# A gated mix of recurrent attention and a GEGLU FFN on one core: down weights in six narrower buffers, turns of x in four banks, earlier first fills, later moved loads, fewer closing waits

## The chip, the cores and the metric

The kernel runs on one core of one Trainium2 chip. The core has engines with instruction streams of their own: TensorE (PE, with its weight loads PEld), VectorE (DVE), ScalarE (ACT), GpSimd (POOL) and SyncE (SP, which here only issues transfers). They share an on-chip buffer and eight accumulation banks of 128 x 512 fp32, numbered 0 to 7. A DMA is issued by an engine (SP, ACT or POOL), and a semaphore says when it has landed. An engine works its stream in order: an instruction that waits holds up everything behind it on that engine.

The metric is the time of one execution on the device in microseconds; less is better. Before the change it is 2202.14 us, the median of 3 runs (2199.84 to 2203.8).

## The reference

Inputs are x (1 x 2048 x 1024), a start memory of 8 rows, attention weights for 32 heads of 128, FFN weights with F = 3584, and gate_w; all bf16. The result mixes a recurrent attention `a` with a feed-forward block `b` by a gate per row:

```python
def _A_ref(x, mem0, Wq, Wk, Wv, Wo, seg_len):          # seg_len 32: 64 segments
    mask = (idx[:, None] < M) | (idx[:, None] >= idx[None, :])
    mem = mem0
    for s in range(n_seg):
        h = jnp.concatenate([mem, xs], axis=1)         # 8 + 32 rows
        q, k, v = (jnp.einsum('btd,dhe->bhte', h, W) for W in (Wq, Wk, Wv))
        scores = jnp.einsum('bhqe,bhke->bhqk', q, k) * scale
        p = _softmax(jnp.where(mask[None, None], scores, -1000000000.0), axis=-1)
        o = jnp.einsum('bhqk,bhke->bhqe', p, v)
        o = jnp.einsum('bhte,hed->btd', o, Wo)
        mem = o[:, :M, :].copy()                       # the next segment's memory
        outs.append(o[:, M:, :])
    return jnp.concatenate(outs, axis=1)

def _B_ref(x, w_gate, w_up, w_down):
    return _gelu(x @ w_gate) * (x @ w_up) @ w_down

g = _sigmoid((x * gate_w).sum(-1, keepdims=True))
return g * a + (1 - g) * b
```

Each segment's memory is the output of the one before it, so the 64 steps are a chain. The three `einsum`s for q, k, v are written as one line here.

## The kernel before

**How the program comes about.** The source builds a list with `op(engine, function, rd=..., wr=..., lane=...)`. From what an operation reads and writes a small planner works out what it must wait for. A `lane` is a semaphore that counts one kind of DMA. There is no scheduler: each engine gets its operations in the order in which the source calls `op`. `emit` writes the streams; at the end SP waits for every lane's last value (`finals`, line 153), 98 lanes in 49 instructions. On POOL each operation that is no DMA waits for the one before it, too.

**FFN first** (loop over `fb`, lines 1053 to 1164): four blocks of 512 tokens. The up phase runs over j = 0 to 27, slices of 128 of F: 8 matmuls with w_gate and 8 with w_up into two banks (line 1068), then gelu and the product on ACT and DVE (1076 to 1084) into `GT[j]`. The down phase has two passes, `ps` = 0 and 1, of two 128-token tiles each, four matmuls per j (line 1134). In blocks 0 to 2 the down weights come in pieces of `WD` = 4 slices (1 MB) through three buffers `wd0` to `wd2`. The first pass takes the pieces forward, the second backward (`back`), so that the last ones are still there. When a piece is done, its buffer is loaded with the piece three further on; in the backward pass at c = 3 SP first issues `load_xT`, the next block's x, turned. In block 3 all down weights lie in `wdF`, filled during its up phase by the table `jF`.

**Turns of x** (`do_x`, 546 to 575): for each 128-token tile T eight transposes on PE write a bank; ACT and DVE copy the bank to `xT` or `xq`; a third copy on DVE takes the 8 last rows of each segment to `hR`, `hR1` or `xr`; `put` writes both to the scratch tensors `xq_scr` and `xr_scr` with DMAs issued by ACT. `dot_x` makes the gate's dot product for T: a product on POOL and a reduction on DVE, one right behind the other. `gate(fb)` turns four of them into sigmoids and stores them to `gt_scr`. Tiles 0 to 3 are turned at the start, later ones in j = 6, 11, 16, 21 of blocks 0 to 2. `tr_mem` transposes the start memory and part of the mask, at the start too.

**The scan** (64 steps) holds what it can of the attention weights in 50 slots of 512 KB, `edge(n)` being the start of slot n. What does not fit is swapped in each step, by SP: a 1.5 MB and a 1 MB load for v, 1 MB each for k and q, and pieces of Wo (`wall`). `walk` is the fixed order of the 64 weight pieces in a step: k, q and v with r = 0, k and q with r = 1, o with r = 0, v with r = 1, o with r = 1, eight numbers n each; r is the half of the heads. `plan(s)` hangs operations on places of the walk: `on("q", 1, 4, f)` runs f just before piece ("q", 1, 4). `begin(n)` issues the first load of slot n, as soon as its bytes in the FFN's layout are free.

For the 8 rows that a segment passes on, keys, queries and values of their x part are worked out ahead for four segments at a time: `fill` (line 907) projects them with a weight half that lies in the slots, `fill_evac` copies the bank to a stage (`X0` to `X3`, `Y0` to `Y2`) and, for v, writes it to `v_scr` (`v_scr puts`, by POOL); `fill_put` turns k or q and writes it to `qk_scr`, by POOL too. Before they are used POOL reads them back: `load_qk` into `qkr`, `load_v` into `vB`. `put_rest` (936) copies the keys from `qkr` behind those of the step (`kT`). `scores` (757) needs this; `attend` has two parts, the second (800) reading `vB`. For step 0 all of these come early: k and q of half 0 in the FFN's last pass, the others in step 0 itself. POOL's order there was load_v(0, half 0), kT copy, fills' stores, load_qk(0, 1), kT copy, load_v(0, half 1).

**The end.** In the last step five Wo pieces, which the closing reads again, are loaded to other places (`late`, lane names moved0 to moved4). The closing (line 1189) multiplies what `o_scr` collected for the 512 passed-on rows (`oR0` to `oR3`, 128 rows each) with Wo, 32 matmuls per half of the columns; DVE mixes (1197) into `orb`, and SP stores it. `blend` mixes the other rows, tile by tile, and ACT stores them. A store of the second half writes the same key `("D", "out", T)` as that of the first, so it waits for it.

The five lines on which the down phase's waits hang:

```python
if back and c == 3:
    load_xT(fb + 1)
nc_ = c - 3 if back else c + 3
if 0 <= nc_ < NWD:
    load_wd(nc_)
```

## Time and profile before

| what | time, us |
| --- | --- |
| median of 3 runs | 2202.14 (2199.84 to 2203.8) |
| profiled execution, own time | 2196.2 |
| its span, first to last instruction | 2194.4 |
| x loaded and turned, first up matmul starts | 11.2 |
| block 0: up, down | 102.56, 53.87 |
| block 1: up, down | 101.36, 49.39 |
| block 2: up, down | 100.42, 50.44 |
| block 3: up; down with the first fills | 96.91; 54.8 |
| step 0 of the scan starts, about | 625 |
| closing, first to last matmul of line 1189 | 2131.27 to 2187.1 |
| last out store issued | 2190.42 |

An "own time" is the device time of the one execution that the profiler took; the span runs from its first to its last instruction, and 1.8 us lie around it. The 64 steps take about 22.9 us each, some 1,506 of the 2,194 us. Over the whole span the page has these totals:

```profile
PE 2033.8 (93%) x31337; PEld 972.6 (44%) x31365; DVE 1027.1 (47%) x2657; ACT 551.6 (25%) x1142; POOL 443.1 (20%) x835
...
DMA packets 180106, 640.23 MB, mean 292 GB/s; under 512 B 25144, under 2 KB 74936, under 8 KB 138976
...
wd<-in_B_w_down_dram SPq DMA_DIRECT2D x27, 1024.0 KB, 6.7
```

The first line gives each engine's busy time, its share and its number of instructions: TensorE is busy for 93% of the span. The last is from the list of DMA issues: 27 loads of down weights of 1 MB, with a median of 6.7 us from issue to landing.

### The profile page before, as it was taken

The page shows a single profiled execution, that of the slowest core. Times are in us where ns is not written, and L with a number is a line of the kernel's source. Part 1 is how long each engine was busy: PE and PEld are TensorE (multiplying, and loading weights), DVE is VectorE, ACT ScalarE, POOL GpSimd, SP SyncE. Part 2 cuts the span into 40 slices and gives each one's busy share as a digit, 9 for nine tenths or more (in the row PEclk, how much of TensorE's full clock was granted, in tenths as well). Part 3 has the DMA queues.
Part 4 walks back from the last instruction along what each step waited for, and adds up shares of the span by engine and source line. Part 5 has one row for each costly group of instructions (what it writes and reads, how often), then busy time and mean ns, then how long its engine had stood idle before and what let it go on. Part 6 is the DMA issues. An engine that isn't in the chain of part 4 may idle for free.

```text
span 2194.4 us, 69744 instructions
## 1 busy us (share of the span) xinstructions
PE 2033.8 (93%) x31337; PEld 972.6 (44%) x31365; DVE 1027.1 (47%) x2657; ACT 551.6 (25%) x1142; POOL 443.1 (20%) x835
## 2 busy tenths in 40 slices
PE   8999999999979899998999999999899999999878
PEld 4444444444434444444444444444444444444345
DVE  5615616436224445444454454544544545445444
ACT  3303303213112222222222222222223222222210
POOL 3000100000022222322223223222232322222110
PEclk9999999999999999999999999999999999999999
DMA  9352264364587999999899999999999999999997
GB/s 308 128 192 89 91 219 124 84 234 165 185 307 285 336 338 344 346 358 345 328 357 348 356 354 342 356 343 360 344 340 349 346 338 358 337 348 347 337 334 269
DMA packets 180106, 640.23 MB, mean 292 GB/s; under 512 B 25144, under 2 KB 74936, under 8 KB 138976
## 3 DMA queue, kind: packets, MB, share of 16 engines
q1 hardware_dynamic: 150800, 595.52, 74.3%
q0 software_dynamic: 17472, 26.41, 3.9%
q10 hardware_dynamic: 11536, 13.85, 1.8%
q8 instruction: 246, 4.03, 0.7%
q14 instruction: 52, 0.43, 0.1%
HBM read 600.00 MB, written 50.27 MB: 296 GB/s over the span
## 4 chain that ended last, share of the span: by engine, by line
PE 65%; DMA 22%; DVE 6%; ACT 3%; issue 2%; POOL 1%; ACTq 0%; SPq 0%; POOLq 0%
PE pb L834 24%; PE pb L1068 14%; DMA wall<-o_scr 9%; PE pb L1134 7%; PE pb L850 5%; PE pb L732 3%; PE pb L867 3%; PE pb L907 3%; PE pb L1189 3%; DMA o_scr<-oRc 2%; DMA sl<-v_scr 2%; DMA wd<-in_B_w_down_dram 2%; DMA qk_scr<-1S 2%; DVE oT L718 1%; DMA v_scr<-kS 1%
## 5 line engine op out<-in xcount | busy, mean ns | idle before, releaser
L834 PE MATMUL pb<-sl,hT 128*32 128x512 bf16 x12288 | 761.8, 382 | 21.4 <-DVE hT L894 8.8
L834 PEld LDWEIGHTS pb<-sl,hT 128*32 128x32 bf16 x12288 | 309.4, 97 | 328.1 <-DVE hT L894 27.6
L907 PE MATMUL pb<-sl,hR 128*32 128x512 bf16 x3072 | 213.5, 384 | 7.1 <-DMA sl<-in_A_Wk_dram 3.8
L1068 PE MATMUL pb<-xT,wg 128*128 128x512 bf16 x896 | 213.4, 381 | 5.4 <-DVE GT L1084 4.1
L1068 PE MATMUL pb<-xT,wu 128*128 128x512 bf16 x896 | 212.5, 380 | 0.0
L817 POOL COPY oRc<-oT 128x128 bf16<-128x128 bf16 x128 | 96.6, 755 | 407.6 <-DVE oT L718 407.6
L867 PE MATMUL pb<-wall,oT 128*32 128x256 bf16 x4056 | 151.0, 278 | 28.4 <-DMA wall<-o_scr 24.5
L1134 PE MATMUL pb<-wd,GT 128*128 128x512 bf16 x657 | 147.2, 382 | 7.1 <-DMA wd<-in_B_w_down_dram 6.3
L718 DVE COPY part<-pb 64x256 f32<-64x256 f32 x96 | 40.4, 421 | 237.3 <-PE pb L867 237.3
L850 PE MATMUL pb<-wall,oT 128*32 128x512 bf16 x2048 | 145.8, 381 | 5.8 <-issue 0.2
L1076 ACT ACTIVATE s<-pb 128x512 f32<-128x512 f32 x112 | 66.8, 596 | 308.8 <-PE pb L1068 269.9
L1077 DVE SCALAR_TENSOR_TENSOR tp<-s,pb 128x512 f32<-128x512 f32 x112 | 76.8, 686 | 131.9 <-ACT s L1076 131.9
L867 PEld LDWEIGHTS pb<-wall,oT 128*32 128x32 bf16 x4056 | 97.4, 97 | 87.8 <-ACT oT L715 26.3
L1068 PEld LDWEIGHTS pb<-xT,wg 128*128 128x128 bf16 x896 | 86.8, 98 | 110.8 <-DVE GT L1084 8.0
L1068 PEld LDWEIGHTS pb<-xT,wu 128*128 128x128 bf16 x896 | 87.9, 98 | 106.6 <-issue 1.6
L768 ACT ACTIVATE E<-pb 128x320 bf16<-128x320 f32 x128 | 56.0, 437 | 311.0 <-DVE pb L767 311.0
L718 DVE COPY kT<-pb 128x512 bf16<-128x512 bf16 x128 | 54.4, 425 | 159.9 <-PE pb L732 159.8
L936 POOL COPY kT<-qkr 128x128 bf16<-128x128 bf16 x128 | 37.2, 291 | 423.1 <-DVE tAB L780 222.9
L715 ACT ACTIVATE oS<-pb 128x512 bf16<-128x512 f32 x63 | 37.6, 597 | 336.0 <-PE pb L834 336.0
L780 DVE STREAM_TRANSPOSE tAB<-pAB 128x128 bf16<-128x128 bf16 x512 | 114.0, 280 | 4.4
L1081 DVE SCALAR_TENSOR_TENSOR tp<-tp,pb 128x512 f32<-128x512 f32 x112 | 77.0, 687 | 78.7 <-ACT tp L1080 78.7
L718 DVE CAST oT<-pb 128x160 bf16<-128x160 f32 x256 | 76.4, 320 | 75.6 <-PE pb L800 75.5
(113 smaller groups left out, 2208.5 us busy)
## 6 DMA issues: line engine op xcount, KB each, us to landing
sl<-v_scr SPq DMA_DIRECT2D x64, 1536.0 KB, 10.0
wall<-o_scr SPq DMA_DIRECT2D x63, 1536.0 KB, 9.2
wall<-o_scr SPq DMA_DIRECT2D x131, 512.0 KB, 5.1
sl<-k_scr SPq DMA_DIRECT2D x64, 1024.0 KB, 5.8
sl<-q_scr SPq DMA_DIRECT2D x64, 1024.0 KB, 8.3
sl<-v_scr SPq DMA_DIRECT2D x64, 1024.0 KB, 9.6
wd<-in_B_w_down_dram SPq DMA_DIRECT2D x27, 1024.0 KB, 6.7
wdF<-in_B_w_down_dram SPq DMA_DIRECT2D x7, 1024.0 KB, 8.9
```

What stands on the lines that cost most here:

```text
L718: op("dve", lambda e: e.tensor_copy(o, i), rd=rd, wr=wr, after=after)
L780: return [op("dve", lambda e, c=c: e.transpose(tAB[:, c + 32 * k:c + 32 * k + 4 * w].rearrange("p (j x) -> p j x", j=4)[:, :, 0:32], pAB[: ...
L817: op("pool", lambda e: e.tensor_copy(oRc[:, :, 16 * u:16 * u + 16].rearrange("p c x -> p x c"), oT[:, :, :, 32:40].rearrange("p g j c -> p ...
L834: ins = e.matmul(PB[bk][32 * g:32 * g + 32, :], lhsT=h[:, i, :], rhs=w[:, g * 512:(g + 1) * 512], start=(n == 0), stop=(n == 7))
L850: ins = e.matmul(PB[XO][32 * g:32 * g + 32, :], lhsT=oT[:, j, x, 0:32], rhs=wall[:, na:nb + 1:nb - na, c:c + 256], start=(n == 0 and hp == 0),
L867: ins = e.matmul(PB[XO][32 * g:32 * g + 32, 256 * b:256 * b + 256], lhsT=oT[:, j, x, 0:32], rhs=w[:, c:c + 256], start=False, stop=(n % 4 ...
L907: ins = e.matmul(PB[b][32 * g:32 * g + 32, :], lhsT=h[:, k[2], :], rhs=w[:, g * 512:(g + 1) * 512], start=(n == 0), stop=(n == 7))
L1068: ins = e.matmul(PB[bk][:, 0:FB], lhsT=w[:, kc, cc:cc + 128], rhs=xT[:, :, :, kc, :].rearrange("p t i c -> p (t i) c"), start=(kc == 0), s ...
L1076: op("act", lambda e, hg=hg: e.activation(s1[:, :], hg, ACTF.Square, scale=SQ), rd=[BK(bg)], wr=[s1.r()])
L1077: op("dve", lambda e, hg=hg, t=t: e.scalar_tensor_tensor(out=t[:, :], in0=s1[:, :], scalar=1.0, in1=hg, op0=ALU.add, op1=ALU.mult), rd=[BK ...
L1081: op("dve", lambda e, hu=hu, t=t: e.scalar_tensor_tensor(out=t[:, :], in0=t[:, :], scalar=1.0, in1=hu, op0=ALU.add, op1=ALU.mult), rd=[BK( ...
L1134: ins = e.matmul(PB[bank[2 * k + hf]][:, :], lhsT=GT[:, j, tb * 128:(tb + 1) * 128], rhs=w[:, x, hf * 512:(hf + 1) * 512], start=(j == end ...
```

## The change

- `emit` goes through the lanes from the one used last backwards and leaves out those whose value is implied by what SP has waited for already (`clock`). `finish` keeps SP's clock for it.
- `WD` is 2 and there are six buffers `wd0` to `wd5`, with the same bytes in all; a piece is 512 KB, a load takes the piece six further on, and `load_xT` is issued at c = 6, behind that step's `load_wd(0)`. `wdF` is filled in 14 pieces instead of 7, in the same three places of the up phase (j = 1, 6, 13).
- Tiles 0 to 3 are turned in banks 4 to 7 instead of 4 and 5 by turns. The third copy of a turn is inside `put`, and `xr_scr` is written by POOL. `dot_x` is split into `dot_m` (POOL), a little earlier, and `dot_r` (DVE), one j later; `gate` into `gate_a` (ACT, j = 25) and `gate_b` (DVE and POOL's stores, j = 27). `tr_mem` and its two copies follow j = 4 of block 0.
- In the layout `xT` lies at slot 41, `wdF` at 27 to 40, `osbF` at 42. Of the slots begun late, 41 comes at the end of block 3's up phase, 27 and on follow one per piece in the last pass, and the last one, now 42 instead of 28, is begun in step 0 at ("q", 0, 4).
- First fills: the v fill of half 0 and `load_v` of half 0 move into the FFN's last pass, with a stage `Y3` in `vB`. In step 0 the k and q fills of half 1 come earlier or in other banks, `load_qk(0, 1)` at ("q", 1, 0) instead of ("q", 1, 4), `load_v` of half 1 at ("o", 0, 0) instead of ("o", 0, 4), which on POOL is ahead of the kT copy that was ahead of it.
- In the last step all five moved loads stand at ("v", 0, 5). Before, three stood at ("q", 0, 4) and two at ("v", 0, 4).
- Each half of an out store has a key of its own.

The diff, cut to its core:

```diff
...
+        self.last = clocks["sp"]
 
     def emit(self, block):
         self.finish()
         by = {e: [o for o in self.ops if o.eng == e] for e in self.ENGS}
-        finals = [(ln[0], ln[1]) for ln in self.lanes.values()]
+        finals, ck = [], dict(self.last)
+        for ln in sorted(self.lanes.values(), key=lambda ln: -ln[2].idx):
+            if ck.get(ln[0], 0) < ln[1]:
+                finals.append((ln[0], ln[1]))
+                for m, v in [*ln[2].clock.items(), (ln[0], ln[1])]:
+                    ck[m] = max(ck.get(m, 0), v)
...
-        WD = 4
+        WD = 2
+        NWB = 6
...
-        wd = [al(f"wd{i}", [128, WD, D]) for i in range(3)]
+        wd = [al(f"wd{i}", [128, WD, D]) for i in range(NWB)]
...
-        xT = al("xT", [128, TB, 4, KC, SEG])
-        assert cur[0] == edge(29)
...
-        assert cur[0] == edge(43)
-        osbF = [al(f"osbF{t}", [128, D], at=edge(28) + 2 * D * t) for t in range(2)]
-        wdF = al("wdF", [128, NJ, D], at=edge(29))
+        assert cur[0] == edge(41)
+        xT = al("xT", [128, TB, 4, KC, SEG])
+        osbF = [al(f"osbF{t}", [128, D], at=edge(42) + 2 * D * t) for t in range(2)]
+        wdF = al("wdF", [128, NJ, D], at=edge(27))
...
-        for n in range(4):
+        for n in range(3):
...
+        stage["Y3"] = al("Y3", [128, 512], at=vB.off)
...
-            b = T % 2 + (4, 4, 0, 4)[T // TB]
+            b = T + 4 if T < TB else T % 2 + (4, 4, 0, 4)[T // TB]
...
-            op("dve", lambda e: e.tensor_copy(to, PBV[b].rearrange("p (k i c) -> p k i c", k=KC, i=4)[:, :, :, NR:SEG]),
-               rd=[BK(b)], wr=[to_r])
-
             def put():
+                op("dve", lambda e: e.tensor_copy(to, PBV[b].rearrange("p (k i c) -> p k i c", k=KC, i=4)[:, :, :, NR:SEG]),
+                   rd=[BK(b)], wr=[to_r])
                 op("act", lambda e: e.dma_start(xq_scr[T, :, :, :], xo[0].rearrange("p i k c -> p i (k c)")),
                    rd=[xo[1](0, 4)], wr=[("D", "xq", T)], lane=f"xw{x2}")
                 if T > 0:
-                    op("act", lambda e: e.dma_start(xr_scr[T], to.rearrange("p k i c -> p (k i c)")),
+                    op("pool", lambda e: e.dma_start(xr_scr[T], to.rearrange("p k i c -> p (k i c)")),
                        rd=[to_r], wr=[("D", "xr", T)], lane=f"xv{x2}")
...
-        def dot_x(T):
+        def dot_m(T):
...
+
+        def dot_r(T):
             op("dve", lambda e: e.tensor_reduce(dl[:, T:T + 1], gp[:, :], AX.X, ALU.add), rd=[gp.r()], wr=[dl.r(T, T + 1)])
...
-            op("sp", lambda e: e.dma_start(wd[c % 3][:, :, :],
+            op("sp", lambda e: e.dma_start(wd[c % NWB][:, :, :],
...
-               wr=[wd[c % 3].r()], lane=f"wd{c % 3}")
+               wr=[wd[c % NWB].r()], lane=f"wd{c % NWB}")
...
-        def gate(fb):
+        def gate_a(fb):
...
+
+        def gate_b(fb):
+            c = slice(TB * fb, TB * fb + TB)
+            r = lambda t: t.r(TB * fb, TB * fb + TB)
...
-        jF = {1: (0, 1), 6: (1, 3), 13: (3, NWD)}
+        jF = {1: (0, 2), 6: (2, 6), 13: (6, NWD)}
...
-        op("pe", tr_mem, rd=[pm.r(), mT.r(), ident.r()], wr=[BK(6)])
-        op("dve", lambda e: e.tensor_copy(mS[:, 72:80], PBV[6][:, 64:64 + NB]), rd=[BK(6)], wr=[mS.r(72, 80)])
-        op("dve", lambda e: e.tensor_copy(memT[:, :], PBV[6][:, 0:64]), rd=[BK(6)], wr=[memT.r()])
...
-            if s == 0:
-                on("v", 0, 0, lambda: fill0("v", 0, B2, "X3"))
...
             if s == 0:
-                on("k", 1, 0, lambda: load_v(0, slice(0, 1)))
+                on("k", 1, 0, lambda: fill0("k", 1, B0, "X0"))
             on("k", 1, 1 if s == 0 else 4, lambda: evac(bank_of["v", 0], vA, "act"))
             if s == 0:
                 on(*('k', 1, 4), lambda: scores(ua, False))
-                on("k", 1, 1, lambda: fill0("k", 1, A1, "X0"))
+                on("k", 1, 4, lambda: fill0("q", 1, A1, "X1"))
                 on(*('q', 1, 2), lambda: attend(ua))
                 on("k", 1, 4, lambda: fill_put("k", 1, 0, "X0"))
-                on("q", 1, 0, lambda: fill0("q", 1, B1, "X1"))
-                on("q", 1, 2, lambda: fill_put("q", 1, 0, "X1"))
-                on("q", 1, 4, lambda: load_qk(0, 1))
+                on("q", 1, 0, lambda: fill_put("q", 1, 0, "X1"))
+                on("q", 1, 0, lambda: load_qk(0, 1))
                 on("q", 1, 4, lambda: fill0("v", 1, B2, "X2"))
                 on("q", 1, 4, lambda: load_r(1) if NG > 1 else None)
-                on("o", 0, 4, lambda: load_v(0, slice(1, 2)))
+                on("o", 0, 0, lambda: load_v(0, slice(1, 2)))
+                on("q", 0, 4, lambda: begin(42))
                 on("v", 1, 4, lambda: begin(49))
...
-                on("q", 0, 4, *late[:3])
-                on("v", 0, 4, *late[3:])
+                on("v", 0, 5, *late)
...
+                if fb == 0 and 0 < j <= TB:
+                    dot_r(j - 1)
                 if fb == 0 and j < TB:
+                    dot_m(j)
                     puts.pop(0)()
-                    dot_x(j)
                     load_x(j + NPX)
                 if fb == 0 and j == TB - 1:
                     load_w(3)
                     load_w(4)
-                    for n in range(3):
+                    for n in range(NWB):
                         load_wd(n)
                 if fb == 0 and j == TB:
-                    gate(0)
+                    op("pe", tr_mem, rd=[pm.r(), mT.r(), ident.r()], wr=[BK(6)])
+                    op("dve", lambda e: e.tensor_copy(mS[:, 72:80], PBV[6][:, 64:64 + NB]), rd=[BK(6)], wr=[mS.r(72, 80)])
+                    op("dve", lambda e: e.tensor_copy(memT[:, :], PBV[6][:, 0:64]), rd=[BK(6)], wr=[memT.r()])
+                    gate_a(0)
                 if fb == NFB - 1 and j == 1:
                     begin_h()
                 T = TB * (fb + 1) + (j - 6) // 5
                 if fb < NFB - 1 and j in (6, 11, 16, 21):
+                    dot_m(T)
                     do_x(T)
-                    dot_x(T)
                     load_x(T + NPX)
+                if fb < NFB - 1 and j in (7, 12, 17, 22):
+                    dot_r(T)
                 if fb < NFB - 1 and j == 25:
-                    gate(fb + 1)
+                    gate_a(fb + 1)
+                if fb < NFB - 1 and j == 27:
+                    gate_b(fb + 1)
+                if fb == 0 and j == TB + 1:
+                    gate_b(0)
                 if fb in (1, 2) and j % 2 == 1:
                     spread(copies.pop(0))
                 if fb == NFB - 1:
...
-                for n in (11, 12, *range(20, 28)):
+                for n in (11, 12, *range(20, 27), 41):
...
                     if not end:
-                        if back and c == 3:
-                            load_xT(fb + 1)
-                        nc_ = c - 3 if back else c + 3
+                        nc_ = c - NWB if back else c + NWB
                         if 0 <= nc_ < NWD:
                             load_wd(nc_)
+                        if back and c == NWB:
+                            load_xT(fb + 1)
                     elif ps == NPS - 1:
-                        for f in {1: [lambda: fill0("k", 0, A0, "Y0")],
-                                  2: [lambda: fill0("k", 0, A1, "Y1", 1, hR1), lambda: fill_put("k", 0, 0, "Y0")],
-                                  3: [lambda: fill0("q", 0, XO, "Y2"), lambda: fill_put("k", 0, 1, "Y1")],
-                                  4: [lambda: fill_put("q", 0, 0, "Y2")], 5: [lambda: load_qk(0, 0)]}.get(c, ()):
+                        for f in {3: [lambda: fill0("k", 0, A0, "Y0")],
+                                  5: [lambda: fill0("k", 0, A1, "Y1", 1, hR1), lambda: fill_put("k", 0, 0, "Y0")],
+                                  7: [lambda: fill0("q", 0, XO, "Y2"), lambda: fill_put("k", 0, 1, "Y1")],
+                                  9: [lambda: fill_put("q", 0, 0, "Y2"), lambda: fill0("v", 0, A0, "Y3")],
+                                  10: [lambda: load_qk(0, 0)], 13: [lambda: load_v(0, slice(0, 1))]}.get(c, ()):
                             f()
-                        for n in (29 + 2 * c, 30 + 2 * c, 43 + c):
-                            if n < 49:
-                                begin(n)
+                        begin(27 + c)
+                        if c % 2 and c < NWD - 1:
+                            begin(43 + c // 2)
...
-        begin(28)
...
-                   rd=[ob.r(lo, hi)], wr=[("D", "out", T) for T in range(4 * b, 4 * b + 4)], lane=f"or{hf}")
+                   rd=[ob.r(lo, hi)], wr=[("D", "out", T, hf) for T in range(4 * b, 4 * b + 4)], lane=f"or{hf}")
...
```

More of the change, by code (lines that the diff above doesn't have):

```diff
@@ L520, in bass_gated_mix__memory_aug_recurrent_mem_tr__geglu_ffn__prompt_kernel @@
             stage[f"Y{n}"] = al(f"Y{n}", [128, 512], at=kT.off + 1024 * n)
+        stage["Y3"] = al("Y3", [128, 512], at=vB.off)
+        assert a_bf.off == vB.off + 512
         tp = [al(f"tp{t}", [128, FB], FP32, at=qkr.off + 4 * FB * t) for t in range(2)]
@@ L1124, in bass_gated_mix__memory_aug_recurrent_mem_tr__geglu_ffn__prompt_kernel @@
                 for c in range(NWD)[::-1 if back else 1]:
-                    w = wdF if end else wd[c % 3]
+                    w = wdF if end else wd[c % NWB]
                     for jj in range(WD)[::-1 if back else 1]:
```

4 lines of the change are left out of this document (2 added, 2 removed).

## The prediction, made before the changed kernel was run

> **What bounds the kernel now.** I read the page's chain and totals, the table by stage, TensorE's waits stage by stage, then single spans. Durations come from the one profiled execution: span 2194.4 us plus 1.8 around it, 2196.2 in all. The median of the three runs, 2202.14, is 5.9 above that; I take every gain off the median unscaled.
>
> ```profile
> PE 65%; DMA 22%; DVE 6%; ACT 3%; issue 2%; POOL 1%; ACTq 0%; SPq 0%; POOLq 0%
> ```
>
> The table by stage has: stretch and length, then busy time and instructions of PE, PEld, DVE, ACT, POOL, then granted clock, DMA share, GB/s.
>
> ```profile
> 114.00:168.00 54.00, 50.15 (x221) 22.02 (x224) 4.10 (x6) 0.00 (x0) 0.00 (x0) 0.97 0.62 205
> 168.00:269.00 101.00, 98.80 (x480) 45.33 (x480) 65.17 (x100) 36.18 (x61) 10.70 (x8) 1.00 0.29 92
> 590.00:625.00 35.00, 33.70 (x274) 15.01 (x279) 6.73 (x11) 1.79 (x3) 2.83 (x4) 1.00 0.91 309
> 625.00:690.00 65.00, 51.35 (x920) 23.00 (x912) 21.33 (x65) 14.81 (x32) 15.58 (x31) 0.89 0.75 267
> 690.00:2090.00 1400.00, 1292.37 (x26615) 623.03 (x26609) 682.66 (x2080) 377.93 (x842) 371.42 (x737) 1.00 0.93 346
> 2131.00:2195.00 64.00, 55.55 (x250) 36.58 (x255) 26.56 (x27) 0.32 (x1) 0.71 (x1) 0.95 0.79 265
> ```
>
> The FFN to about 620 is bound by TensorE, with holes. The scan from 690 to 2090 runs against its transfers (93%, 346 GB/s), and no edit touches its steady steps. So whatever the change is worth lies in four places: the up phases, the down phases, the transition 590 to 690 (13.65 us without a matmul, the two rows' sum) and the last 90 us. The waits of TensorE, 0 to 170 us (us in total, times, longest):
>
> ```profile
> PE pb L1134 <- DMA wd<-in_B_w_down_dram: 3.6, 2, 2.2
> PE pb L1068 <- DVE GT L1084: 1.2, 1, 1.2
> ```
>
> The same view from 625 to 700:
>
> ```profile
> PE pb L757 <- POOL kT L936: 5.1, 1, 5.1
> PE pb L907 <- DMA sl<-in_A_Wk_dram: 3.8, 1, 3.8
> PE pb L800 <- DMA vB<-v_scr: 1.7, 1, 1.7
> PE pb L907 <- DMA sl<-v_scr: 1.5, 1, 1.5
> ```
>
> The timeline (start, duration, instruction, idle time before it and its releaser):
>
> ```profile
> 162.46 5.31 PE L1134 MATMUL pb<-wd,GT 128*128 128x512 bf16 x16 [2.18 <-DMA wd<-in_B_w_down_dram]
> 214.49 1.49 ACTq L570 DMA_DIRECT2D xr_scr<-xr  x1
> 219.50 1.90 PE L1068 MATMUL pb<-xT,wg 128*128 128x512 bf16 x8 [1.92 <-DVE GT L1084]
> 2124.75 1.04 PE L834 MATMUL pb<-sl,hT 128*32 128x512 bf16 x8 [5.89 <-DMA sl<-v_scr]
> 2188.08 0.54 SPq L1200 DMA_DIRECT2D out_dram<-orb  x1
> 2190.42 0.54 SPq L1200 DMA_DIRECT2D out_dram<-orb  x1
> ```
>
> **A. Turns of x, the gate's dots: 1.2 us.** At the start a third turn waits 0.20 for the copy at L563; four banks and the copy's move into put() take that away: up to 0.23. Against it, tr_mem (0.45 of TensorE) now stands between j=4 and j=5. It was ahead of L1068's start before, but there beside copies. In the first five j of block 0, VectorE has 0.69+0.63+0.69+0.69+1.21 = 3.9 us of work per j against 3.45 of matmuls; the moved copy (0.28) makes it 4.2. The 1.21 us wait at 46.56 came from ScalarE's 2.56 us issue of xr at 40.47, now POOL's; I credit the block +0.2 in all. In block 1 the 1.49 us issue above held up s(12) until 216.03 and so the matmul at 219.50. That issue goes to POOL, which is idle there, and the 1.21 reduce goes into the next j, so the stall shrinks by about 1.0. In block 2 (stall 0.97, issue only 0.54) I expect nothing. Bounds: all four, 0.23+1.21+1.92+0.97 = 4.3; below, -1.0 if VectorE's chain stops TensorE in each early j.
>
> **B. Down weights in 512 KB pieces over six buffers: 7.0 us.** The three down phases last 53.87, 49.39 and 50.44. The second less its three waits (0.20, 0.23, 0.30) is a clean 48.66, so 5.2+0.7+1.8 = 7.7 are lost: waits of 1.47 (125.52), 2.18 (162.46), 1.94 (465.76), and 16 matmuls that took 5.31 instead of 3.63 at half clock behind the second. A 1 MB piece issued at 117.17 took 8.3 us to land, one at 153.41 9.0, behind the xT load; three buffers allow about 7. Now a buffer comes free every 8 matmuls (1.73 us), and five further pieces cover a load for 8.7 us. The bytes are the same; needed is 512 KB per 1.73 us, and eleven 512 KB weight loads issued at 469.4 to 474.6 landed 1.27 to 1.5 us apart. xT is asked for three matmul groups later and still has some 2 us in hand. The gate's 4-byte DMAs now lie beside the first loads. I keep back 0.7 for that and the spread copies, so 7.0; bounds 4.5 (only the three waits less 1) and 7.7.
>
> **C. Transition: +0.3 us.** The v fill and part of the v loads move into the FFN's last pass, and slot 42 takes the place of slot 28 in the queue. Before, SP stood 4.7 us (629.57 to 634.29) at slot 28, waiting for osbF's stores; k's swap landed at 636.89, v3's at 646.83. After, with the same bytes and with dips of about 1.75 us closed, I put k's swap at 633.8, v3's at 645.1: the v fill's wait goes, and the 3.8 shrinks to 2.5. But step 0's scores hang on POOL's queue in order: put q, load_qk (now at q,1,0), load_v(0,1:2), then the kT copy. The vB load now stands ahead of put_rest on POOL; it waits for the v puts, which land behind the three wall loads that SP issued 1 to 2 us before. By the spacing of 1.28 us per 512 KB they land at about 658.2, the copy ends at 658.9, scores start at 659.1: a wait of 9.8 instead of 5.08, while the waits for hR (0.87), a memset (1.35) and vB (1.69) fall away. The second attend, 664.04 before, comes at 663.7. Hence +0.3. Bounds: -4.6 if put q also lands behind the walls, +7 if POOL's small DMAs do not queue behind SP's large ones at all.
>
> **D. Last step and end: 4.0 us.** The V swap was issued at 2109.47 behind five moved loads (2106.38 to 2108.80), and TensorE waited 5.89 for it. Without 5x1.28 us ahead of it v3 lands at 2118.2 where 2118.9 is needed: the wait goes. But oR0, first operand of L1189, lands at about 2128.3 in either order, so L1189 starts at 2128.3 instead of 2131.27: 3.0 at most. Even that does not reach the end as it stands:
>
> ```profile
> 2173.45 0.75 DVE L1197 SCALAR_TENSOR_TENSOR orb<-pb,gR,brb 128x512 bf16<-128x512 f32 x1 [11.89 <-DMA out_dram<-orb]
> ```
>
> VectorE waits there for the first out store, landed behind a full queue of loads, and works without a gap to 2186.41. Only the hole in the transfers around 2130 to 2135 (0.69 share, 1.5 us) can close, since gR's issue waits less; I take 1.0 of it. Firm is the end: the second half's store waited for the first's landing (2188.08, 2190.42; now 0.6 apart: 1.76), and 49 final wait instructions, some 60 ns each,
>
> ```profile
> L153 SPq EVENT_SEMAPHORE  x49: 28/28/28, 2191.0 to 2193.9; - x49
> ```
>
> run on after the last landing at 2192.70; two remain: 1.26. Sum 3.0 firm, plus 1.0. Bounds: 2.5 (some waits run beside the landing anyway) and 8.9 (all of the 5.89 carried, plus 3.0).
>
> **Sum.** 1.2+7.0+0.3+4.0 = 12.5: own time 2196.2-12.5 = 2183.7, median 2202.14-12.5 = **2189.6 us**.
>
> **Rivals.** (1) The transition gains too: POOL's small DMAs are served beside the large ones; put k lands at 642.4, the v puts at 648.5, vB at 651, the kT copy is done at 652: C is +7, total 19.2, 2182.9. For it: hardly anything. Against it: a_scr's 64 KB, issued by POOL at 2106.12, 0.11 after SP's 1.5 MB v swap, landed after 9.04 us, 0.5 before the swap's 2115.64. The Trainium skill (DMA: Bandwidth & Descriptors, section "Queues, rings and completion order") says that each engine goes round between its queue rows packet by packet, which is what this rival supposes; the a_scr row does not look like it, as 64 KB served by turns would not need 9 us. A larger share of packets for POOL than that row shows would be needed.
>
> (2) POOL's chain loses: v3 stays late because osbF's stores land after v0's swap, or put q falls behind the walls: C is -4.6, total 7.6, 2194.5. For it: SP's 4.7 us at slot 28 shows how late those stores land. Against: the v fill has less to do after 625.
>
> (3) Slower: 512 KB loads of wd do not overlap. Alone, such a load takes 3.8 us (469.42 to 473.23, first of its batch). A pass has eight loads behind its six in place: 8x3.8 = 30.4 against 12x1.73 = 20.8 us of cover, 9.6 lost in each of six passes, 57 in all and 7.7 won: about 2251. It decides from 2.6 us per load on, and the total is slower from about 2.9 (8x0.3x6 = 14). Against it: the spacing of 1.27 to 1.5 us when several are in flight. The Trainium skill (same page, section "Bandwidth") has the rule to batch transfers to 1 MiB or more for 75% of peak, which speaks against halving; 512 KB per 1.28 us is 410 GB/s here, so the trace does not bear it out.
>
> (4) The front's gain is hidden: the saturated transfers (91% from 590 on) end when they did, the scan starts as before, and only D's firm 3.0 stay: 2199.1. Against: these transfers are issued at points of TensorE's program and move with it.
>
> **Chances.** Forecast 0.53, rivals in order 0.20, 0.12, 0.09, 0.06. Range 2181 to 2199: it takes in the forecast's bounds but for their far ends, rival 2 and most of rival 1, and leaves out rival 3. Differences below 0.2% (4.4 us) can't be told from none in three runs. Faster by more: 0.53+0.20+0.10 = 0.83; within: 0.08 (rival 4, 0.02 of rival 2); slower: 0.09.
>
> **What will show it.** B: no wait of L1134 for wd, all three down phases at 48.7. A: at block 1's j=13 a stall of about 0.9, not 1.92. C: the kT wait before step 0's scores near 10 us with vB's wait gone (rival 1: below 3). D: no wait for v3 in the last step, L1189 some 3 us earlier against the scan's end, yet the last blends no earlier than 1 us; the last two stores about 0.6 apart, two closing waits. Wrong it would be by waits for wd that stay, or by a kT copy past 662.

## The result, and the profile after

The changed kernel takes 2211.1 us (median of 7 runs, 2207.78 to 2215.9). The kernel before, run beside it, takes 2197.14 (7 runs, 2193.25 to 2203.8). The ratio is 1.0061 with a 95% interval of 1.0043 to 1.0079: the change made the kernel slower by 14 us, where 12.5 us faster was forecast, and the time lies outside the forecast range of 2181 to 2199. The profiled executions show the same difference: a span of 2209.4 us against 2194.4.

The chain of waits of the changed kernel has more DMA in it (24% against 22%) and less TensorE:

```profile
PE 61%; DMA 24%; DVE 6%; ACT 3%; issue 2%; SPq 2%; POOL 1%; ACTq 0%; DVEq 0%; POOLq 0%
```

Laid over each other, the two traces differ by these stretches (us; the marks are the first up matmul, the starts of the up and down phases, the first `o_scr` store of the scan and the last k swap):

| stretch | before | after | difference |
| --- | --- | --- | --- |
| to the first up matmul | 11.18 | 10.47 | -0.7 |
| up phases of blocks 0 to 2 | 304.34 | 303.42 | -0.9 |
| down phases of blocks 0 to 2 | 53.87, 49.39, 50.44 | 55.08, 55.37, 56.00 | **+12.75** |
| up phase of block 3 | 96.91 | 96.91 | 0 |
| last down phase, to the first o store (transition) | 99.6 | 103.4 | +3.9 |
| first o store to the last k swap (scan) | 1436.2 | 1439.2 | +3.0 |
| last k swap to the end | 92.5 | 89.5 | -3.0 |

The sum is +15.0. No edit touches the steady steps of the scan, and the seventeen profiles of this case have 1436 to 1452 us for it, so its +3.0 is scatter; the transition scatters too, as shown below. Only the down phases stand clear of it. The table by stage of the changed kernel (stretch, length; busy time and instructions of PE, PEld, DVE, ACT, POOL; granted clock, DMA share, GB/s) shows the down phases in its first three rows, the transition and the end in the last two:

```profile
114.00:168.00 54.00, 48.99 (x216) 21.68 (x219) 2.75 (x5) 0.00 (x0) 4.25 (x5) 0.94 0.71 195
269.00:319.00 50.00, 45.48 (x196) 20.04 (x199) 3.65 (x8) 0.00 (x0) 4.26 (x5) 0.93 0.66 188
419.00:470.00 51.00, 46.01 (x198) 20.09 (x201) 7.12 (x13) 2.45 (x4) 2.65 (x5) 0.93 0.59 153
625.00:690.00 65.00, 47.89 (x713) 20.61 (x712) 15.43 (x42) 9.90 (x20) 14.90 (x28) 0.84 0.71 247
2131.00:2210.00 79.00, 66.91 (x471) 42.18 (x469) 33.01 (x49) 3.09 (x9) 2.73 (x5) 0.95 0.87 291
```

The granted clock of the down phases is 0.93 to 0.94 (before: 0.97 in the first). TensorE stands still in each of them, and around the end of each wait the trace has half the clock for 6.8 us (0.52 on the mean from 126 to 133 us). Its waits from 100 to 490 us (total, times, longest) say for what it stands:

```profile
PE pb L1151 <- DMA wd<-in_B_w_down_dram: 13.9, 3, 4.8
PE pb L1074 <- DVE GT L1090: 2.9, 6, 0.9
```

The waits for down weights, which the six buffers were forecast to end, are one of 4 to 5 us in each block. The timeline of the first one (start, duration, instructions, idle time and releaser):

```profile
113.90 19.12 SPq L627 DMA_DIRECT2D wd<-in_B_w_down_dram  x8
114.32 2.12 POOL L654 DMA_DIRECT2D gt_scr<-gal  x4 [20.21 <-DVE gal L651]
...
129.02 4.31 PE L1151 MATMUL pb<-wd,GT 128*128 128x512 bf16 x10 [4.80 <-DMA wd<-in_B_w_down_dram]
```

SP starts its loads at 113.90, and 0.42 us later POOL issues the gate's four stores of 128 numbers of 4 bytes, now at j=27. The first load landed after 3.84 us. The second, issued at 115.63, landed at 128.98, after 13.35; the stores landed at 125.4 to 127.7, and the next five loads 1.3 to 1.4 us apart behind the second. That explains the size of the wait: the five pieces in place cover 8.7 us, as the prediction had it, and 13.35 less 8.7 is 4.7, where TensorE waited 4.80. The second loads of blocks 1 and 2 took 12.87 and 13.34, which leaves 4.2 and 4.7, and the waits are 4.31 and 4.78. In block 1 the view of the transfers while the stores were under way (274 to 282 us), and behind them (284 to 290), each line from a view of its own:

```profile
DMA packets 202, 0.34 MB, mean 42 GB/s; under 512 B 37, under 2 KB 37, under 8 KB 202
```

```profile
DMA packets 1203, 2.31 MB, mean 386 GB/s; under 512 B 76, under 2 KB 76, under 8 KB 1202
```

With SP's loads waiting in the queue all the time, 42 GB/s moved beside the stores and 386 after them.

In the transition the wait for kT before step 0's scores became 10.8 us, as the prediction had it (9.8), but the other waits did not shrink enough to pay for it (632 to 690 us):

```profile
PE pb L766 <- POOL kT L945: 10.8, 1, 10.8
PE pb L916 <- DMA sl<-k_scr: 3.9, 1, 3.9
PE pb L916 <- DMA sl<-v_scr: 1.7, 1, 1.7
```

At the end, one wait instruction is left of 49 (source line 159 is `emit`'s last wait; columns are duration in ns, first and last start):

```profile
L159 SPq EVENT_SEMAPHORE  x1: 17/17/17, 2208.3 to 2208.3; - x1
```

### The profile page after: what moved, and what is told of

It reads as the page before. It is cut to its first block, busy times and chain, and to the rows that moved or that the text cites. A ratio compares the mean times of both kernels' runs of the same rounds, so it can differ in the third digit from the quotient of the medians.

```text
span 2209.4 us, 69729 instructions
## 1 busy us (share of the span) xinstructions
PE 2044.6 (93%) x31337; PEld 977.5 (44%) x31365; DVE 1026.9 (46%) x2657; ACT 551.2 (25%) x1142; POOL 450.8 (20%) x850
## 3 DMA queue, kind: packets, MB, share of 16 engines
q10 hardware_dynamic: 9376, 12.87, 1.7%
## 4 chain that ended last, share of the span: by engine, by line
PE 61%; DMA 24%; DVE 6%; ACT 3%; issue 2%; SPq 2%; POOL 1%; ACTq 0%; DVEq 0%; POOLq 0%
PE pb L843 22%; PE pb L1074 13%; DMA wall<-o_scr 11%; PE pb L1151 8%; PE pb L859 5%; PE pb L741 3%; PE pb L876 3%; PE pb L916 2%; DMA o_scr<-oRc 2%; DMA qk_scr<-1S 2%; DMA wd<-in_B_w_down_dram 2%; DMA sl<-v_scr 1%; DVE oT L727 1%; PE pb L801 1%; DMA v_scr<-kS 1%
## 5 line engine op out<-in xcount | busy, mean ns | idle before, releaser
L1151 PE MATMUL pb<-wd,GT 128*128 128x512 bf16 x657 | 152.4, 393 | 14.7 <-DMA wd<-in_B_w_down_dram 13.9
L1151 PEld LDWEIGHTS pb<-wd,GT 128*128 128x128 bf16 x672 | 67.3, 101 | 99.8 <-DMA wd<-in_B_w_down_dram 15.4
```

Of the source, the lines that this page charges most:

```text
L1151: ins = e.matmul(PB[bank[2 * k + hf]][:, :], lhsT=GT[:, j, tb * 128:(tb + 1) * 128], rhs=w[:, x, hf * 512:(hf + 1) * 512], start=(j == end ...
```

## The experiments

Theory 1 is that the gate's small stores hold up the loads of wd; theory 2 that the 512 KB pieces or their order are slow by themselves. All edits are to the changed kernel unless said otherwise. Each run was taken beside the kernel before, whose median there was 2202 to 2206 us; its ratio is to be laid beside the 1.0061 of the changed kernel. Down phases are those of blocks 0, 1, 2, from the one profile of each run.

**e1_gate_early**

```diff
-                if fb < NFB - 1 and j == 25:
+                if fb < NFB - 1 and j == 23:
                     gate_a(fb + 1)
-                if fb < NFB - 1 and j == 27:
+                if fb < NFB - 1 and j == 24:
                     gate_b(fb + 1)
```

> The changed kernel with one edit: gate_a stands at j=23 instead of 25 and gate_b, with its four 128 x 4-byte stores, at j=24 instead of 27, in blocks 0 to 2. Theory 1 (the gate's small stores block the loads of wd that share the DMA engines with them): the stores are done before the down phase, the waits of L1151 for wd (4.80, 4.31, 4.78) go, the three down phases fall from 55.08, 55.37 and 56.00 to about 48.7 each, and the time falls by some 20 us to about 2191. Theory 2 (the 512 KB pieces over six buffers are slow by themselves): the waits stay, about 2211.

Measured: 2186.49 us (6 runs) against 2202.24 for the kernel before (23), ratio 0.9935 (0.991 to 0.9961). The down phases are 48.35, 48.35, 48.35, and in TensorE's waits from 100 to 470 us the line for wd is gone:

```profile
PE pb L1074 <- DVE GT L1090: 2.9, 6, 0.9
```

Theory 1 gave the number, theory 2 did not. Three j earlier the stores land at 110.3 to 112.4, when the first phase begins at 110.2.

**e2_before_gate27** (the kernel before)

```diff
-                if fb < NFB - 1 and j == 25:
+                if fb < NFB - 1 and j == 27:
                     gate(fb + 1)
```

> The kernel before with one edit: gate(fb+1) at j=27 instead of 25, so that its four small stores are issued at the start of the down phase; the down weights stay in three 1 MB buffers. Theory 1: the first load of wd in each down phase lies behind the stores and lands some 4 to 6 us late; the three down phases (53.87, 49.39, 50.44) grow to about 55 to 58, together +10 to +15 us, about 2208 to 2212. Theory 2: nothing changes, 2197.

Measured: 2232.78 us (4 runs) against 2202.24, ratio 1.0149 (1.0125 to 1.0174): slower by twice what theory 1 had. The phases are 64.23, 62.38, 62.52, with nine waits for wd (TensorE from 100 to 520 us):

```profile
PE pb L1134 <- DMA wd<-in_B_w_down_dram: 36.2, 9, 9.5
```

So the late stores are enough without six buffers. With 1 MB pieces the first load of the phase lies behind the stores (in block 0 it took 13.1 us, and three buffers cover about 7), and the waits come back at the next piece and in the second pass; six narrower buffers made the loss smaller, not larger.

**e3_before_six** (the kernel before with the down weights in six narrower buffers and nothing else)

```diff
-        WD = 4
+        WD = 2
+        NWB = 6
...
-            op("sp", lambda e: e.dma_start(wd[c % 3][:, :, :],
+            op("sp", lambda e: e.dma_start(wd[c % NWB][:, :, :],
```

The fills and slot loads of the last pass are hung on the 14 pieces at the places they had before.

> The kernel before with the down weights in 512 KB pieces over six buffers and xT asked for at c=6, and nothing else; the gate stays at j=25. Theory 1: the pieces alone give what the prediction had for them, down phases near 48.7 in blocks 1 and 2, and block 0, where the stores of j=25 still reach into the phase, 49 to 52: 4 to 7 us faster, about 2190 to 2193. Theory 2: the down phases become about 55 as in the changed kernel, some 10 us slower, about 2208.

Measured: 2194.26 us (12 runs) against 2202.24, ratio 0.9962 (0.9943 to 0.9981), phases 48.35, 48.35, 48.35 with the gate where it was. The line for wd is gone here too (TensorE from 100 to 470 us):

```profile
PE pb L1069 <- DVE GT L1085: 2.1, 3, 0.9
```

The stores of j=25 were still under way when this run's loads began: in block 0 the first load, issued at 113.89, took 7.9 us, and the longest first load of the three phases took 8.2. The pieces in place cover 8.7, so nothing waited. Relative to the start of the phase, the change issues the stores some 7 us later, and that carried the hold-up past the cover. The 7.0 that the prediction gave this part are borne out: the runs differ by 8.0 us, the profiled phases by 8.65, 5.5 of them in block 0.

**e10_before_gate23** (the kernel before, gate at j=23 instead of 25)

```diff
-                if fb < NFB - 1 and j == 25:
+                if fb < NFB - 1 and j == 23:
                     gate(fb + 1)
```

> The kernel before with one edit: gate(fb+1) at j=23 instead of 25. If its own waits for wd (1.47, 2.18, 1.94) were partly the work of the same stores, which at j=25 landed at 121.1, 273.5 and 423.8, after the down phases began at 113.7, 269.0 and 418.8: the first waits of blocks 0 and 2 go, and of the phases' 7.7 us above 48.66 some 3 to 5 go. If they come from three buffers of 1 MB alone: phases as before, and no change of time.

Measured: 2197.65 us (10 runs) against 2203.23, ratio 0.9974 (0.9951 to 0.9997). Phases 50.64, 49.06, 50.67: of the 8.65 us that the old phases had above 48.35, 3.3 went, among them the whole first wait of block 0. So the stores cost the old kernel something too: the 1 MB load that took 8.3 us in block 0, a row that the prediction read as the price of 1 MB pieces, took 5.4 here. The rest (waits of 2.1 in the second passes) came from three 1 MB buffers.

**e4_before_close** (the kernel before with the end alone)

```diff
-        finals = [(ln[0], ln[1]) for ln in self.lanes.values()]
+        finals, ck = [], dict(self.last)
...
-                   rd=[ob.r(lo, hi)], wr=[("D", "out", T) for T in range(4 * b, 4 * b + 4)], lane=f"or{hf}")
+                   rd=[ob.r(lo, hi)], wr=[("D", "out", T, hf) for T in range(4 * b, 4 * b + 4)], lane=f"or{hf}")
```

> The kernel before with the end alone changed: the closing waits thinned and a key for each half of an out store. The prediction's firm term: the last two stores some 0.6 apart instead of 2.3, two waits instead of 49 behind the last landing, 3.0 us off the end, about 2194. Rival: the waits run beside the landing and the receipt anyway, and at most 1.7 us goes.

Measured: 2200.64 us (12 runs) against 2202.24, ratio 0.9993 (0.9967 to 1.0019). The runs can't tell 3 us from none. The traces can: from the start of VectorE's last mix to the end of the span before, e2 and e3 have 7.25, 7.71 and 8.26 us, after, e1 and e4 4.8 to 4.9; and from the last k swap to the end the four profiles with the old end (before, e2, e3, e10) have 93.7 on the mean, e4 90.9.

**e6_stores_later and e8_one_store**: the stores put later in the source, all four or three of them.

```diff
+        def gate_s(fb):
...
             for T in range(TB * fb, TB * fb + TB):
                 op("pool", lambda e, T=T: e.dma_start(gt_scr[4 * T:4 * T + 4, :, :].rearrange("s r o -> (s r) o"), gal[:, T:T + 1]),
...
+                if fb > 0 and j == 3:
+                    gate_s(fb)
```

> The changed kernel, with gate_a at j=25 and gate_b's two VectorE operations at j=27 as they are, and only the four stores moved, to j=3 of the next block's up phase. Theory 1 (the stores themselves hold up the loads of wd): down phases near 48.4, about 2187 to 2191. Rival (what hurts is the rest of the gate's work at the end of the up phase): phases of 55 to 56, about 2211.

> The changed kernel with one of the four stores left at j=27 and three moved to j=3 of the next block. If the hold-up grows with the number of stores: it is a quarter of some 9 us for the second load of wd, which the five pieces in place cover: no wait, phases near 48.4, about 2189. If one such store is enough: waits of 4 to 5 us as in the changed kernel, about 2211.

Measured: 2209.57 (10 runs) against 2204.34, ratio 1.0024 (1.0001 to 1.0047), and 2210.7 (10), ratio 1.0041 (1.002 to 1.0062). Waits for wd stayed, 18.0 us in e8 and 12.9 in e6:

```profile
PE pb L1157 <- DMA wd<-in_B_w_down_dram: 12.9, 3, 4.6
```

That seemed to go against theory 1, but the trace shows that the edit moved nothing: POOL has no other work there, so it reaches the stores early, finds the gate's values ready and issues them at 112.85 to 114.43, while the loads start at 112.42. A later place in the source holds an idle engine back by nothing. The next two runs repeat both with a real dependency:

**e6b_stores_wait and e8b_one_store**

```diff
+                if fb > 0 and j == 3:
+                    for T in range(TB * fb + 0, TB * fb + TB):
+                        gate_s(T, (made,))
```

(`made` is VectorE's last operation of j=3 in the next block; e8b leaves the first store free at j=27 and begins this range one higher.)

> As e6_stores_later, but each of the four stores is also made to wait for VectorE's last operation of j=3 in the next block, since in e6 POOL, with nothing else to do, issued them at the same time as before (112.85 to 114.43). Theory 1 (the stores themselves): no store beside the loads of wd, down phases near 48.4, about 2187 to 2191. Rival (the rest of the gate's work at the end of the up phase): 55 to 56, about 2208.

> As e6b, but one of the four stores stays free at j=27 and three wait for the next block. If the hold-up grows with the number of stores: the second load of wd lands some 2 to 3 us late, the pieces in place cover it, no wait, phases near 48.4, about 2189. If one store of 128 x 4 bytes is enough: a wait of 3 to 5 us in each down phase, about 2205.

Measured: e6b 2183.61 us (5 runs) against 2203.23, ratio 0.9914 (0.9883 to 0.9945), phases 48.38, 48.35, 48.35, with the gate's computation still at j=25 and 27 (TensorE from 100 to 470 us):

```profile
PE pb L1077 <- DVE GT L1093: 2.9, 6, 0.9
```

So it is the stores, not the gate's other work. e8b 2208.96 (10 runs), ratio 1.0018 (0.9993 to 1.0043), phases 52.82, 55.24, 56.25: three quarters of the stores gone, and nearly the whole loss is still there.

```profile
PE pb L1157 <- DMA wd<-in_B_w_down_dram: 11.4, 3, 4.8
```

The one store in block 0 was issued at 112.87 and landed at 122.36, and the second load of wd took 11.2 us (12.5 and 13.4 in blocks 1 and 2), the first, issued at 112.45, 3.9. In e6b, without stores, the second load took 4.6 to 4.8. The hold-up hardly grows with the number of stores: with four, in the changed kernel, the second load took 12.9 to 13.4.

**e7_stores_act**

```diff
-                op("pool", lambda e, T=T: e.dma_start(gt_scr[4 * T:4 * T + 4, :, :].rearrange("s r o -> (s r) o"), gal[:, T:T + 1]),
+                op("act", lambda e, T=T: e.dma_start(gt_scr[4 * T:4 * T + 4, :, :].rearrange("s r o -> (s r) o"), gal[:, T:T + 1]),
```

> The changed kernel with the four stores at j=27 issued by ScalarE instead of POOL. If it is POOL's way of making transfers that holds up the loads: down phases near 48.4, about 2190. If 128 writes of 4 bytes hold up the engines whoever issues them: the waits for wd stay within 1 us of 4.80, 4.31 and 4.78, about 2211.

Measured: 2207.06 us (10 runs) against 2204.34, ratio 1.0019 (0.9995 to 1.0043), phases 54.37, 55.53, 53.82. The waits for wd are six instead of three, 13.6 us in all against 13.9:

```profile
PE pb L1151 <- DMA wd<-in_B_w_down_dram: 13.6, 6, 4.0
```

It is not POOL's way of issuing: even the load issued ahead of the stores (115.06) now took 12.6.

**The transition.** The next runs start from e1. The stretch is the transition of the table, from the last down phase to the first o store; e1 has 97.0. Each has one profile, and seven profiles whose transition is the same code have 94.0 to 103.4, so these runs show which wait ends last, but no gain or loss of the stretch. Their times can't be told from e1's either.

e5_vb_behind:

```diff
-                on("o", 0, 0, lambda: load_v(0, slice(1, 2)))
+                on("o", 0, 2, lambda: load_v(0, slice(1, 2)))
```

> e1_gate_early with one more edit: load_v of half 1 in step 0 at (o,0,2) instead of (o,0,0), so that on POOL it stands behind put_rest's kT copy. Theory (the in-order POOL): in e1 the copy came at 643.73 behind the vB load issued at 643.18, although qkr had landed at 637.00; now the copy is done near 638 and the 4.53 us before step 0's scores become less than 1, of which some 2 us come back as a wait for vB (landed at 648.25): from the last FFN pass to step 0's o store 97.0 becomes about 95, and the time about 2184. Rival: vB ends the stretch anyway, the wait only changes its name, 97 and 2186.5.

Measured: 2190.7 us (9 runs) against 2204.34, ratio 0.9935 (0.9913 to 0.9956), the stretch 96.9. No wait for kT is left, and a wait for vB of 3.2 is there instead. The rival was right: the wait changed its name.

e11_slot42_later:

```diff
-                on("q", 0, 4, lambda: begin(42))
+                on("k", 1, 1, lambda: begin(42))
```

> e1_gate_early with begin(42) at (k,1,1) instead of (q,0,4), so that on SP's queue it stands behind the second v swap. In e1 SP waited at slot 42 for osbF's stores until 627.15 and issued that swap at 627.58, after v0's 1.5 MB had landed at 627.15; it landed at 633.80 and TensorE waited 3.99 us. Theory (SP's queue in order): the swap is issued near 615, lands some 2.6 us behind v0, near 630, the wait falls below 1 us, and from the last FFN pass to step 0's o store 97.0 becomes 93 to 94; the time 2183. Rival (the transfers are full, what is ahead of one wait moves the next): 97 with a longer wait for kT or vB, 2186.

Measured: 2189.19 us (8 runs) against 2203.23, ratio 0.993 (0.9901 to 0.9959). The v swap was issued at 617.97 and TensorE no longer waits for it, as the theory had it, but the stretch is 100.4, longer than in e1 (97.0):

```profile
PE pb L766 <- POOL kT L945: 10.8, 1, 10.8
PE pb L916 <- DMA sl<-k_scr: 4.1, 1, 4.1
```

SP issues the three wall loads at 636.84 to 638.27, the first of them 2.9 us earlier behind the start of the last down phase than in e1, and POOL's load_qk, issued at 640.74, 3.7 later than in e1 by the same count, lands behind two of them, at 647.31 (the third, of 1.5 MB, at 647.55).

e12_put_lanes, and e14_lanes_vb (e12 with e5's edit):

```diff
-               rd=[st.r()], wr=[("D", "qk", G, m, u)], lane="fq")
+               rd=[st.r()], wr=[("D", "qk", G, m, u)], lane=f"fq{m}")
```

> e1_gate_early with a semaphore of its own for the k puts and the q puts (lane fqk, fqq instead of fq), so that step 0's q put no longer waits until the k put has landed. In e1 the k put was issued at 626.97, landed at 631.37, and the q put was issued at 631.92. Theory (b): the q put is issued 3 to 4 us earlier, load_qk and the v puts land ahead of the wall loads, and the kT wait of 4.53 falls to 1 to 2: last FFN pass to step 0's o store from 97.0 to about 94, time 2183. Theory (c): 97 and 2186.

> e12 with load_v of half 1 behind the kT copy as in e5. Theory (a)+(b): no kT wait, a vB wait of at most 2: about 93 to 94 and 2183. Theory (b) alone: as e12.

Measured: e12 2188.05 (7 runs) against 2205.99, ratio 0.9918 (0.989 to 0.9946), stretch 94.0 without a kT wait; e14 2186.92 (6), ratio 0.9923 (0.9895 to 0.9952), stretch 96.6 with a vB wait of 2.4. In e12 the q put was indeed issued 0.9 us behind the k put, but both then landed only with the v swap (636.25), at 636.1 and 636.4, so load_qk (636.73) came no earlier in the step than in e1. What differs is that the first wall load came 0.7 us behind the last v put (640.61) instead of 0.1 in e1, and all four v puts had landed by 641.7, where in e1 the last one landed 4.2 us behind the others. e6b, with the transition's code untouched, also has 94.0, so this run does not show that the second semaphore helps.

e13_all: e11 with both edits.

> e11_slot42_later with both edits. In e11 the second v swap came in time, but the wall loads then were issued at 636.84 to 638.27, ahead of load_qk (640.74), and kT waited 10.76. Theory (a)+(b): with the q put issued 3 to 4 us earlier load_qk comes about with the first wall load and the copy hangs on it alone: the kT wait falls to some 4 us, a vB wait of 2 to 4 stays: 100.4 becomes about 94 and the time 2183. Theory (c): 100 and 2189.

Measured: 2181.71 us (6 runs) against 2205.99, ratio 0.9899 (0.9875 to 0.9922), the stretch 94.2 instead of e11's 100.4. load_qk (632.61) was issued 0.4 ahead of the first wall load, and in place of e11's one wait of 10.8 there are three of 1.6 to 4.4, beside the k swap's:

```profile
PE pb L916 <- DMA hR<-xr_scr: 4.4, 1, 4.4
PE pb L916 <- DMA sl<-k_scr: 1.7, 1, 1.7
PE pb L809 <- DMA vB<-v_scr: 1.7, 1, 1.7
PE pb L766 <- POOL kT L945: 1.6, 1, 1.6
```

It has the lowest median of all, faster than both kernels; from e1, e5, e6b, e11, e12 and e14 the intervals don't separate it.

## Why the prediction was wrong, point by point

**B, the down weights: wrong, and most of the miss.** Of the 27.5 us between forecast and profiled pair 19.8 are here; 4.2 are the transition and 3.0 the scan, both within their scatter. The step that failed is the sentence "The gate's 4-byte DMAs now lie beside the first loads. I keep back 0.7 for that and the spread copies". The place was seen, the size was not: 12.75 us were lost in the profiled pair where 7.0 should have been won. One such store beside the loads costs 2.6 to 4.8 us of waiting per block (e8b), and the half clock that goes with the wait adds to it: in the changed kernel's block 0 the phase is 6.7 longer than 48.35, of which 4.8 is the wait. The rest of the term came out: without the stores beside the loads (e1, e6b), or with the gate left at j=25 (e3), the phases are 48.35, somewhat better than the clean 48.66 that the sum was made with. But 3.3 of the old phases' 8.65 were the stores' work (e10) and not, as the term had it, that of three 1 MB buffers.

The trace of before had the price, in a row that I used for something else. Block 0's four gate stores were issued at 34.58 to 36.44 and landed at 47.3 to 49.5. From 36 to 47 us the view shows two stores of ordinary size and the last two of the gate's:

```profile
xq_scr<-xq ACTq DMA_DIRECT2D x1, 256.0 KB, 12.5
xr_scr<-xr ACTq DMA_DIRECT2D x1, 64.0 KB, 12.9
gt_scr<-gal POOLq DMA_DIRECT2D x2, 0.5 KB, 12.7
```

The same xq store takes 2.0 to 6.4 us elsewhere in that trace. I read the 2.56 us issue at 40.47 as ScalarE's cost of issuing, and did not ask why two transfers of 64 and 256 KB landed only behind the small stores, at 52.6 and 53.4, and why from 40 to 46 us, with loads of up weights queued, only 53 to 73 GB/s moved.

That halving the pieces does the harm was rival 3. It is refuted: the Trainium skill's rule to batch transfers to 1 MiB (DMA: Bandwidth & Descriptors, section "Bandwidth") was cited for it, and in e1, e3 and e6b 512 KB pieces leave no wait for wd at all.

**A, the turns: not contradicted.** Forecast 1.2, measured 1.6 in the pair. Over all profiles, start and three up phases together are 313.5 on the mean of the five with the old turns and 312.6 on that of the seven with the change's turns and transition unaltered (after, e1, e6, e6b, e7, e8, e8b): 0.9. But the five spread from 312.4 to 315.5 and the seven from 311.4 to 315.0, so that the 1.2 was met is not shown, only that nothing large came of it. The wait in block 1 that was to fall from 1.92 to about 0.9 is 0.86; e3, with the old turns, has 0.87, so the turns are not shown to be its cause.

**C, the transition: the kT wait was right, the sum is not shown.** kT's copy hung on POOL's queue as forecast (10.8 against 9.8), and the wait for vB was gone. But the 3.8 for the k swap, put at 2.5, is 3.9, and the wait for the v fill's weights that was to go (1.5) is 1.7. The old transition is 99.2 to 100.4 us in five profiles. The new one, the same code in those seven profiles, is 103.4, 97.0, 99.7, 94.0, 97.0, 99.5 and 101.8, a mean of 98.9: forecast 0.3 faster, measured 0.9, with about the spread that the bounds of -4.6 and +7 gave. With that spread the agreement of the means is luck as much as reckoning. What decides is rival 2's point, whether POOL comes behind SP's wall loads. In after and e8b load_qk was issued 1.4 and 1.1 us behind the first wall load, and kT waited 10.8 and 10.3; in the other five it was issued 1.0 to 3.7 ahead of it, and kT waited 6.1 at most. e11 puts POOL 3.9 behind and has 10.8. Rival 1, POOL's transfers served beside SP's large ones, has no run for it: behind the first wall load, load_qk took 6.2 to 7.2 us to land (after, e8b, e11), ahead of it 2.1 to 2.3.

**D, the end: right.** Forecast 4.0. From the last k swap to the end the four profiles with the old end have 92.5 to 95.4, mean 93.7; the twelve with the new end and the moved loads behind the V swap have 89.0 to 90.6, mean 89.7. e4, the end alone, has 90.9, so some 2.8 are the stores and the closing waits (3.0 forecast) and 1.2 the moved loads (1.0), as far as one profile of e4 can tell. The 5.89 wait did go, and L1206 starts 26.9 us behind the last k swap instead of 29.4, but the blends are tied to transfers, as forecast. The moved loads alone were not run.

**Readings of the prediction that don't hold.** "13.65 us without a matmul, the two rows' sum" is the row 625 to 690 alone; the two rows give 14.95. The 4.7 us from 629.57 to 634.29 are not SP standing at slot 28 but that slot's load on its way; SP stood before it, some 8 us from 621.34 on, for osbF's stores, and issued k's swap at 629.96. The eleven loads landed 1.27 to 1.5 us apart but for one gap of 2.13. The first and the third change no term; the second was one of C's premises and rival 2's ground.

**The sum.** Without the stores beside the loads, e1 is 15.75 us below the kernel before (8.6 to 19.8 by the interval) and e6b 19.6 (12.1 to 25.8); the sum said 12.5. One sentence of one term turned it round.

## What to carry to other kernels

- A transfer of few bytes is not a small transfer. Before moving one, look in the trace at what else was in flight beside it and how long that took to land; here 512 bytes in 128 pieces held up a load by 6.5 us (block 0: 11.2 in e8b against 4.7 for the same load in e6b), which at 386 GB/s is the time of 2.5 MB.
- On an engine with nothing else to do, a later place in the program moves nothing: to hold a store back, give it something to wait for, and check in the trace when it was issued.
- Where two queues race for the same engines, one profile is one outcome. Compare the same stretch in every profile at hand before giving a gain or a loss to an edit there.

## What the runs showed of the hardware

While stores of 128 x 4 bytes were under way, little of the loads issued behind or just ahead of them moved: 36 to 56 GB/s in the three blocks of the changed kernel and 48 to 57 in those of e8b, with one store, for 6 to 10 us, against 386 after them. ScalarE's stores held them up as long as POOL's (e7). Why is open: in the trace of the changed kernel the loads' 2 KB packets between 270 and 283 us take 0.27 us on the mean and 6.4 at most (0.09 and 0.64 between 284 and 290), but nothing shows what they wait for. The stores' own packets are soon through: in e8b's block 0 the store's 16 packets of 32 bytes start between 115.40 and 115.97 and take 0.01 us each, yet it landed only at 122.36. (ScalarE's stores in e7 come as 128 packets of 4 bytes each.) No run writes the same 512 bytes in larger pieces, so that the small pieces are the reason is likely but not shown. The Trainium skill (DMA: Bandwidth & Descriptors, section "Specifications") says that a transfer below 512 B is done by reading, modifying and writing; that would make such stores slow, but no run here shows why loads into the chip's buffer are slowed with them.
